# Spreading the attention's reciprocals by DMA through DRAM instead of by TensorE, in a linear-attention and MLP block on one Trainium2 core

## The chip, the cores and the metric

The kernel runs on 1 core of one Trainium2 chip. The metric is the device time of one execution in microseconds (us). Before the change it was 215.84 us, the median of 4 runs (215.45 to 216.13).

The engines are called by the profile's names: PE is TensorE, DVE is VectorE, ACT is ScalarE, POOL is GpSimd, and SP is the engine whose queue issues the DMAs.

## The reference, cut to what matters

```python
# x: 2048 tokens x 640; 32 heads of 20; everything bf16
xn  = layernorm(x)
q, k, v = heads(xn @ wqkv)                    # 32 heads
pq, pk  = phi(q), phi(k)                      # phi(t) = (t > 0 ? t + 1 : exp(t)) + 1e-6
kv  = einsum("bhsd,bhse->bhde", pk, v)
z   = einsum("bhsd->bhd", pk)
num = einsum("bhqd,bhde->bhqe", pq, kv)
den = einsum("bhqd,bhd->bhq", pq, z)[..., None] + 1e-6
out = x + (num / den) @ wo + gelu(xn @ w1 + b1) @ w2 + b2
```

The division is by one number per head and token. The kernel multiplies `pq` by `1/den` before it is used, so each of the 32 reciprocals of a token is needed on 20 partitions of `pqT` (features on partitions, tokens along the row).

## The kernel before: the parts that matter here

PE does, in this order: K, Q and h (the first MLP product) for token groups 0 to 2; K and Q for group 3; G (`xn` transposed times `pk`, 640 x 640) with z, den and the spreading between its parts; h of group 3 with kv, KVW (kv times `wo`) and more spreading between; and the output pass. That pass runs 32 accumulations, each of 12 matmuls of h with `w2` and 5 of `pqT` with KVW.

```python
    # den[32 i + h, s]: denominators of token group i; a reciprocal by Ln and Exp on ACT
    nc.scalar.activation(out=lnden, in_=den[:], func=ACT.Ln, bias=tiny_t[:], scale=1.0)
    nc.scalar.activation(out=recT[:], in_=lnden, func=ACT.Exp, scale=-1.0)

    def emit_pqs(c):                 # spread each reciprocal over the 20 partitions of its head
        rps = [bank() for _ in range(NG)]
        for i in range(NG):
            q = slice(i * H, (i + 1) * H)
            nc.tensor.matmul(
                rps[i][:], lhsT=Em4[q, c * P : (c + 1) * P], rhs=recT[q, :], start=True, stop=True
            )
        for i in range(NG):
            gs = slice(i * TOK, (i + 1) * TOK)
            nc.vector.tensor_tensor(out=pqT[:, c, gs], in0=pqT[:, c, gs], in1=rps[i][:], op=ALU.mult)

    emit_pqs(0)
    emit_Ga(3)                       # G's wide part: 16 matmuls of 512 columns
    emit_pqs(1)
    emit_Gb(3)                       # G's narrow part: 16 matmuls of 128 columns
    ...                              # [cut] pqs(2) in G; h(3), kv, KVW; pqs(3), pqs(4) in h(3)
```

`Em4` is a mask with 32 rows per token group, so the four matmuls of `emit_pqs` each read 32 partitions, where those of G and h read 128 (the trace's forms: 32x512 against 128x512). In the code `P` is 128, `H` the 32 heads, `DH` their 20 features, `NG` the 4 token groups of `TOK` = 512 tokens, `NC` the 5 blocks of 128 features, and `HALF` 320 columns. A bank is a piece of PSUM, the memory that matmuls write to here, and an eviction is the copy of a result out of it. The "products" are the multiplications of `pqT` by the spread reciprocals on DVE.

## Time and profile before

| reading | value | view |
|---|---|---|
| span of the profiled run | 214.0 us | page |
| PE busy | 208.9 us, 98% | page, part 1 |
| chain that ended last, on PE | 95% | page, part 4 |
| PE's waits in total | 2.3 us, all before 9 us | waits of PE |
| end of Q to the output pass | 94.35 to 137.34 us: 42.99 us | chain in order of time |
| granted clock | 1.00 | windows |

From the page of the kernel before: PE's row of part 1, then three rows of part 2, where each digit is the busy share of a fortieth of the span in tenths (PEclk is the granted clock).

```profile
PE 208.9 (98%) x1412; PEld 119.9 (56%) x1412; DVE 100.2 (47%) x249; ACT 83.6 (39%) x135; POOL 60.6 (28%) x82
PE   7799999999999999999999999999999999999994
PEclk9999999999999999999999999999999999999999
DMA  5999970000000000000000000000100110000011
```

PE has no free slice, and the DMA engines are nearly idle after a sixth of the run. So work taken from PE is worth its full time, and DMA has time to give.

The waits of PE, kernel before: engine and line, whom it waited for, total us, times, longest.

```profile
PE mm L183 <- DVE hT L130: 1.1, 1, 1.1
PE mm L272 <- DMA wqk<-in_A_wqkv_dram: 0.9, 1, 0.9
PE mm L248 <- DVE xn L232: 0.3, 1, 0.3
```

All three lie in the start. The chain in order of time, kernel before: start us, us, engine and line, count. L403 is G's wide part, L412 its narrow part, L452 the spreading, L324 is h, and L536 the output pass.

```profile
94.35 3.45 PE mm L403 x16
97.80 0.89 PE mm L412 x16
...
108.81 0.33 PE mm L452 x4
109.14 3.56 PE mm L403 x16
112.70 0.33 PE mm L452 x4
113.03 1.00 PE mm L412 x16
...
132.15 0.33 PE mm L452 x4
132.48 1.19 PE mm L324 x5
...
137.34 1.63 PE mm L536 x12
```

Four spreading matmuls take 0.33 us together. The group behind them is slower than its twins elsewhere: 3.56 instead of 3.45, 1.00 instead of 0.89, 1.19 instead of 1.08 us. The cost of the spreading is therefore not 5 x 0.33 us alone.

### The profile page before, as it was taken

The page shows a single profiled execution, that of the slowest core. Times are in us where ns is not written, and L with a number is a line of the kernel's source. Part 1 is how long each engine was busy: PE and PEld are TensorE (multiplying, and loading weights), DVE is VectorE, ACT ScalarE, POOL GpSimd, SP SyncE. Part 2 cuts the span into 40 slices and gives each one's busy share as a digit, 9 for nine tenths or more (in the row PEclk, how much of TensorE's full clock was granted, in tenths as well). Part 3 has the DMA queues.
Part 4 walks back from the last instruction along what each step waited for, and adds up shares of the span by engine and source line. Part 5 has one row for each costly group of instructions (what it writes and reads, how often), then busy time and mean ns, then how long its engine had stood idle before and what let it go on. Part 6 is the DMA issues. An engine that isn't in the chain of part 4 may idle for free.

```text
span 214.0 us, 3486 instructions
## 1 busy us (share of the span) xinstructions
PE 208.9 (98%) x1412; PEld 119.9 (56%) x1412; DVE 100.2 (47%) x249; ACT 83.6 (39%) x135; POOL 60.6 (28%) x82
## 2 busy tenths in 40 slices
PE   7799999999999999999999999999999999999994
PEld 2454455544554445545554563577777777777762
DVE  4679950999449970794044426612112112112111
ACT  3476769577885869741312736500000000000000
POOL 1000049920550019089899990000000000000000
PEclk9999999999999999999999999999999999999999
DMA  5999970000000000000000000000100110000011
GB/s 175 383 369 312 366 267 5 2 0 0 0 3 0 0 0 3 0 3 0 3 0 0 22 0 0 3 31 31 34 31 31 41 54 31 34 31 31 31 64 31
DMA packets 10079, 12.94 MB, mean 60 GB/s; under 512 B 2304, under 2 KB 8912, under 8 KB 10064
## 3 DMA queue, kind: packets, MB, share of 16 engines
q1 hardware_dynamic: 10064, 12.72, 17.6%
q8 instruction: 11, 0.18, 0.4%
q14 instruction: 4, 0.03, 0.0%
HBM read 10.10 MB, written 2.62 MB: 59 GB/s over the span
## 4 chain that ended last, share of the span: by engine, by line
PE 95%; DMA 3%; SPq 1%; issue 0%; DVE 0%
PE mm L324 24%; PE mm L536 24%; PE mm L540 10%; PE mm L315 10%; PE mm L403 8%; PE mm L272 8%; DMA wqk<-in_A_wqkv_dram 3%; PE mm L412 2%; PE mm L282 2%; PE mm L241 2%; PE mm L452 1%; PE mm L515 1%; PE mm L484 1%; SPq L108 1%; PE mm L439 1%; PE mm L520 0%
## 5 line engine op out<-in xcount | busy, mean ns | idle before, releaser
L536 PE MATMUL mm<-w,hT 128*128 128x320 bf16 (+2 forms) x384 | 57.4, 299 | 0.0
L324 PE MATMUL mm<-xnT,w 128*128 128x512 bf16 x240 | 54.1, 379 | 0.0
L536 PEld LDWEIGHTS <-hT 128*128 128x128 bf16 x384 | 37.1, 98 | 15.3
L544 DVE TENSOR_TENSOR late<-mm,x_all 128x320 bf16<-128x320 f32 (+2 forms) x32 | 15.7, 492 | 58.5 <-PE mm L540 58.5
L328 ACT ACTIVATE hT<-mm,b1col 128x512 bf16<-128x512 f32 x48 | 32.4, 686 | 16.0 <-PE mm L324 15.3
L324 PEld LDWEIGHTS <-w 128*128 128x128 bf16 x240 | 22.8, 98 | 26.6 <-issue 0.7
L256 ACT ACTIVATE e<-mm 128x512 bf16<-128x512 f32 x40 | 23.0, 596 | 12.3 <-PE mm L315 5.4
L540 PE MATMUL mm<-late,pqT 128*128 128x320 bf16 (+2 forms) x160 | 27.0, 299 | 0.0
L257 DVE TENSOR_SCALAR e<-e 128x512 bf16<-128x512 bf16 x40 | 15.0, 374 | 21.5 <-ACT e L256 21.5
L315 PE MATMUL mm<-xnT,wqk 128*128 128x512 bf16 x100 | 22.2, 379 | 0.0
L395 POOL TENSOR_TENSOR x_all<-x_all,b2b 128x640 bf16<-128x640 bf16 x16 | 21.7, 1385 | 0.0
L272 PE MATMUL mm<-wqk,xnT 128*128 128x512 bf16 x80 | 20.4, 379 | 0.9 <-DMA wqk<-in_A_wqkv_dram 0.9
L306 POOL TENSOR_TENSOR zacc<-zacc,pk 128x640 f32<-128x640 f32 x13 | 18.2, 1397 | 7.2 <-DVE pk L260 6.4
L457 DVE TENSOR_TENSOR pqT<-pqT,mm 128x512 bf16<-128x512 bf16 x20 | 12.3, 682 | 14.6 <-PE mm L452 14.6
L540 PEld LDWEIGHTS <-pqT 128*128 128x128 bf16 x160 | 15.5, 98 | 6.3
L403 PE MATMUL mm<-pk,xn 128*128 128x512 bf16 x80 | 18.1, 379 | 0.0
L378 POOL COPY Z3t<-xn 128x1 bf16<-128x1 bf16 x3 | 0.6, 187 | 57.9 <-DVE xn L232 57.9
L315 PEld LDWEIGHTS <-wqk 128*128 128x128 bf16 x100 | 9.6, 98 | 10.8
L196 DVE BATCH_NORM_STATS2 stats<-x_all 128x6 f32<-128x320 bf16 x32 | 13.7, 466 | 3.4 <-DMA x_all<-in_A_x_dram 3.4
L260 DVE SCALAR_TENSOR_TENSOR pk<-mm,e 128x512 bf16<-128x512 f32 x20 | 13.8, 692 | 1.0
L260 DVE SCALAR_TENSOR_TENSOR pqT<-mm,e 128x512 bf16<-128x512 f32 x20 | 13.8, 692 | 0.7
L403 PEld LDWEIGHTS <-xn 128*128 128x128 bf16 x80 | 7.5, 97 | 9.2 <-issue 0.7
(73 smaller groups left out, 132.4 us busy)
## 6 DMA issues: line engine op xcount, KB each, us to landing
w<-in_B_w_dram SPq DMA_DIRECT2D x2, 1920.0 KB, 11.0
out_dram<-late SPq DMA_DIRECT2D x15, 160.0 KB, 1.8
x_all<-in_A_x_dram SPq DMA_DIRECT2D x3, 640.0 KB, 11.1
wqk<-in_A_wqkv_dram SPq DMA_DIRECT2D x1, 800.0 KB, 7.5
wv<-in_A_wqkv_dram SPq DMA_DIRECT2D x1, 800.0 KB
woA<-in_A_wo_dram SPq DMA_DIRECT2D x5, 160.0 KB, 7.4
wqk<-in_A_wqkv_dram SPq DMA_DIRECT2D x1, 480.0 KB, 5.0
x_all<-in_A_x_dram SPq DMA_DIRECT2D x2, 160.0 KB, 2.3
```

The costliest lines, as they stand in the source:

```text
L256: nc.scalar.activation(out=e[:], in_=ps[:], func=ACT.Exp)
L260: nc.vector.scalar_tensor_tensor(out=dst, in0=shaped(ps), scalar=0.0, in1=shaped(e), op0=ALU.max, op1=ALU.add)
L272: nc.tensor.matmul(K_ps[t][:], lhsT=xnT[:, k, t * P : (t + 1) * P], rhs=wqk[:, k, D : D + TOK], start=(k == 0), stop=(k == NC - 1),)
L306: nc.gpsimd.tensor_tensor(out=zsum if u == NT - 1 else zacc[:], in0=pk[:, 0, :] if u == 1 else zacc[:], in1=pk[:, u, :], op=ALU.add,)
L315: nc.tensor.matmul(ps[:], lhsT=wqk[:, k, m * P : (m + 1) * P], rhs=xnT[:, k, gs], start=(k == 0), stop=(k == NC - 1),)
L324: nc.tensor.matmul(ps[:], lhsT=w1[:, k, j * P : (j + 1) * P], rhs=xnT[:, k, g * TOK : (g + 1) * TOK], start=(k == 0), stop=(k == NC - 1),)
L328: nc.scalar.activation(out=hT[g][:, j, :], in_=ps[:], func=ACT.Gelu_apprx_tanh, bias=b1col[:, j : j + 1], scale=1.0)
L395: nc.gpsimd.tensor_tensor(out=x_all[:, t, :], in0=x_all[:, t, :], in1=b2b[:], op=ALU.add)
L403: nc.tensor.matmul(ps[:], lhsT=w, rhs=pk[:, t, 0:TOK], start=(t == 0), stop=(t == NT - 1))
L536: nc.tensor.matmul(ps, lhsT=hT[g][:, j, i * P : (i + 1) * P], rhs=w2[:, j, ns], start=(j == 0), stop=False)
L540: nc.tensor.matmul(ps, lhsT=pqT[:, c, t * P : (t + 1) * P], rhs=KVW[:, c, ns], start=False, stop=(c == NC - 1),)
L544: nc.vector.tensor_tensor(out=osb[:, ns], in0=ps, in1=x_all[:, t, ns], op=ALU.add)
```

## The change

The intent: take the spreading from PE. The reciprocal now goes to DRAM, each row written 20 times by a DMA that reads its source again and again, and comes back as a 640 x 2048 matrix that lies as `pqT` does, into the memory of `xnT`, which is no longer needed then. To have time for that trip, den is computed early, within h of group 3, which moves ahead of G. The rest follows from this: PSUM banks are handed out by hand so that some can be held; z's last adds go to DVE; the reciprocal is a DVE instruction; POOL's 16 bias adds wait (`gate`) for the last product; KVW is made in two halves with held output accumulations between them. The core of the diff, cuts marked:

```diff
+    def emit_den():
+        ...                                        # [cut] the same 20 matmuls as before
+        nc.vector.tensor_scalar(out=zacc[:, 0:TOK], in0=den[:], scalar1=1e-6, scalar2=None, op0=ALU.add)
+        nc.vector.reciprocal(out=recT[:], in_=zacc[:, 0:TOK])
+        for i in range(NG):
+            nc.sync.dma_start(
+                out=rec_rows[:, i * TOK : (i + 1) * TOK].rearrange("(h r) s -> h r s", r=DH),
+                in_=recT[i * H : (i + 1) * H, :].unsqueeze(1).to_broadcast((H, DH, TOK)),
+            )
@@ h of the last group now runs ahead of G
+            if g == 3 and j == 0:
+                emit_zacc(3, nc.vector)
+            if g == 3 and j == 4:
+                emit_z()
+            if g == 3 and j == 5:
+                emit_den()
@@
-    emit_pqs(0)
-    emit_Ga(3)
-    ...                                            # [cut] and all other emit_pqs
+    emit_Ga(0)
+    for c in range(NC):
+        nc.sync.dma_start(out=xnT[:, c, :], in_=rec_rows[c * P : (c + 1) * P, :])
+        nc.vector.tensor_tensor(out=pqT[:, c, :], in0=pqT[:, c, :], in1=xnT[:, c, :], op=ALU.mult)
+    emit_emask()
+    gate(pqT[:, NC - 1, 0:1])                      # a one-element copy on POOL
+    for t in range(NT):
+        nc.gpsimd.tensor_tensor(out=x_all[:, t, :], in0=x_all[:, t, :], in1=b2b[:], op=ALU.add)
+    emit_Gb(0)
+    for j in range(1, NC):
+        emit_G(j)
@@
+    emit_hw(0, halves[0], hold=True)               # 12 matmuls of h with w2 for tile 0
+    emit_KVW(halves[0])
+    emit_hw(0, halves[1], hold=True)
+    emit_KVW(halves[1])
+    emit_hw(1, halves[0], hold=True)
+    emit_hw(1, halves[1], hold=True)
```

## The prediction

> **What bounds it now.** TensorE. The page has PE busy 98% of the 214.0 us span; the chain of waits is 95% PE; the PE waits sum to 2.3 us, all before 9 us. Granted clock is 1.00. A 512-column matmul costs 0.216 us (groups of five, 1.08 us), 320 columns 0.136 us. So only removed PE work, or a new PE wait, moves the time.
>
> **What the change removes, adds, moves.** The denominator's reciprocal is no longer spread over 20 partitions per head by TensorE (mask times recT, 20 matmuls) but by DMA through DRAM: four broadcast writes (2.6 MB), five loads (2.6 MB), five wide DVE products. The last group's h matmuls move ahead of G, den ahead of G too, half of KVW behind first-pass output matmuls; PSUM banks are handed out explicitly.
>
> PE ledger, read from the chain by time. Before, from the end of Q (94.35) to the output pass (137.34): 42.99 us. After, the same work: h 12 x 1.08 = 12.95, z 0.10, den 1.19, G 5 x (3.45 + 0.89) = 21.7, kv 2.06, KVW about 2.2: 40.2. Saved: 2.8 us: 5 x 0.33 us of removed matmuls, and about 1 us because the matmuls after a 32-row group run slower (3.56 instead of 3.45, 1.19 instead of 1.08, 1.00 instead of 0.89). All of it lies on the critical path: floor about 213.1 us.
>
> **What may take it back.**
> 1. den ends near 102.1 us. DVE add 0.7 us, then the reciprocal: not in this trace[...]. Writes start near 106. [...] this trace's loads into 128 partitions made 352 to 382 GB/s (windows view). At about 200 GB/s: 13 us plus latency of about 2 (a 160 KB store takes 1.8 us to land), done near 121; loads at 360 GB/s another 9 us, near 130.5; last product (1.2 us, estimate) near 132. The in-order DVE evicts kv behind these products; PE wants kv near 134.0. Slack only 1 to 2 us; lateness beyond that is lost 1:1.
> 2. woB's loads start when G ends (before: 2.5 us issue plus 1.7 us landing, so 4.2 us); KVW wants them 4.4 us after G: 0 to 0.5 us.
> 3. kv follows G directly, so it waits for G's last eviction on ACT (0.27 us): about 0.3 us.
>
> zsum's four DVE adds (0.82 us each, from 0.49 us at 320 and 0.69 at 512 columns) end near 99.3, before PE wants them at 99.75. The bias adds on POOL (1.385 us each) start late, near 132, but outrun the output pass (2 x 2.31 us a tile).
>
> **Prediction.** 213.6 us, 8 in 10 within 212.6 to 217.0. Faster by over 2%: 0.03; within 2%: 0.90; slower: 0.07.
>
> **What would show it.** Right: PE waits still small after 9 us; removed line gone from PE; output pass ends unchanged; Q ends at 94.35 as before; G near 130.3; 512-column rows at 0.216 us throughout. DMA row busy from about 106 to 131. Wrong on 1: a PE wait of microseconds ahead of the first KVW matmuls, named DVE, with DVE waiting on the load of the spread reciprocal. Wrong on 2: the wait is for the woB DMA.
>
> **What would make it wrong.** Writes well below 200 GB/s (1 KB pieces, 20 readings of a partition) or a slower reciprocal push the time beyond 217; PSUM banks handed out in an unlucky order cost waits inside h or KVW; a PE rate that changes when G runs unbroken.

## The result, and the profile after

The changed kernel took 213.5 us, the median of 10 runs (213.07 to 214.17), against 215.75 us for the kernel before (15 runs, 215.22 to 216.13). The ratio is 0.990, with a 95% interval of 0.9888 to 0.9911. Ratios here are the mean time of one kernel's fast runs over that of the other's of the same rounds, so they are not quite the ratio of the medians quoted. The output is correct. The predicted time was 213.6 us.

The waits of PE after the change are a single line:

```profile
PE bank L180 <- DVE hT L139: 1.1, 1, 1.1
```

The chain in order of time, changed kernel. L318 is den, L353 h, L438 and L447 are G's wide and narrow parts, L487 is kv, L518 is h with `w2`, L537 and L541 are KVW.

```profile
100.41 1.19 PE bank L318 x20
101.61 6.58 PE bank L353 x30
108.19 3.45 PE bank L438 x16
111.64 0.89 PE bank L447 x16
...
129.92 1.40 PE bank L487 x25
131.32 0.66 PE bank L497 x24
131.98 1.74 PE bank L518 x12
133.72 0.68 PE bank L537 x5
134.39 0.37 PE bank L541 x5
134.77 1.74 PE bank L518 x12
...
137.56 3.37 PE bank L518 x24
```

The spreading is gone and G runs at 3.45 and 0.89 us throughout. Four groups are slower than their twins, though, and I had not put that into my sum: h behind den (6.58 us for 30, where 6 x 1.08 = 6.48), and three stretches of h with `w2`, one behind kv's L497 and two behind KVW's L541 (twice 1.74 instead of 1.63, once 3.37 instead of 2 x 1.63 = 3.26 us).

The other side of the bargain is the trip through DRAM. First the DVE timeline of the changed kernel (start us, us, engine, line, operation, tiles, count, idle time before it), then SP's, then three windows (stretch; its length, then for PE, PEld, DVE, ACT and POOL the busy us; granted clock, DMA share, GB/s):

```profile
102.38 3.35 DVE L326 RECIPROCAL recT<-zacc 128x512 bf16<-128x512 f32 x1
125.24 2.46 DVE L463 TENSOR_TENSOR pqT<-pqT,xnT 128x2048 bf16<-128x2048 bf16 x2 [19.50 <-DMA xnT<-rec_rows]
129.29 2.47 DVE L463 TENSOR_TENSOR pqT<-pqT,xnT 128x2048 bf16<-128x2048 bf16 x2 [0.18 <-DMA xnT<-rec_rows]
131.68 0.68 DVE L504 TENSOR_TENSOR late<-bank,zacc 128x512 bf16<-128x512 f32 x1
```

```profile
105.76 6.14 SPq L328 DMA_DIRECT2D rec_rows<-recT  x4
121.13 3.24 SPq L462 DMA_DIRECT2D xnT<-rec_rows  x5
```

```profile
108.00:112.00 4.00, 4.00 (x27) 2.09 (x26) 0.00 (x0) 1.01 (x2) 3.54 (x12) 1.00 0.96 189
112.00:116.00 4.00, 4.00 (x30) 2.11 (x28) 0.00 (x0) 0.26 (x1) 2.50 (x7) 1.00 0.97 209
124.00:128.00 4.00, 4.00 (x32) 2.27 (x30) 2.57 (x3) 1.17 (x2) 0.00 (x0) 1.00 0.98 326
```

The writes go out at 189 to 209 GB/s with the DMA engines 96 to 97% busy, the loads come back at 326. The last product ends at 131.76 us, and the kv eviction (L504) follows at once. PE wants kv at 133.72 us (L537); the eviction of its first four blocks ends at 132.36. The trip fits with 1.36 us to spare.

The start of a run is noisy: in the profiles whose waits were read, PE waited 0 to 1.0 us there for a load of `wqk`. The time from the start of the last eviction to the end of the span varies as well: 2.7 us before the change, 3.2 us after it. For a finer comparison I also give, for each profile, the **inner time**: from the first matmul of Q of group 0 to the start of the last eviction, both read from the chain. The two lines of the kernel before, then the two of the changed kernel:

```profile
14.27 5.39 PE mm L315 x25
211.27 0.29 DVE late L544
13.71 5.40 PE bank L344 x25
208.33 0.29 DVE late L530
```

Before it was 211.27 - 14.27 = 197.00 us, after 208.33 - 13.71 = 194.62 us, so 2.38 us less.

### The profile page after: what moved, and what is told of

Read it like the earlier page. It is cut to its first block, busy times and chain, and to the rows that moved or that the text cites. A ratio compares the mean times of both kernels' runs of the same rounds, so it can differ in the third digit from the quotient of the medians.

```text
span 211.5 us, 3437 instructions
## 1 busy us (share of the span) xinstructions
PE 207.2 (98%) x1392; PEld 120.1 (57%) x1392; DVE 97.1 (46%) x238; ACT 82.7 (39%) x134; POOL 48.5 (23%) x70
## 4 chain that ended last, share of the span: by engine, by line
PE 94%; DMA 2%; DVE 1%; SPq 1%; ACT 0%; issue 0%
PE bank L518 25%; PE bank L353 25%; PE bank L526 10%; PE bank L344 10%; PE bank L438 8%; PE bank L269 7%; DMA x_all<-in_A_x_dram 2%; PE bank L447 2%; PE bank L279 2%; PE bank L238 2%; PE bank L487 1%; PE bank L537 1%; PE bank L318 1%; DVE stats L193 0%; SPq L117 0%; PE bank L541 0%
## 5 line engine op out<-in xcount | busy, mean ns | idle before, releaser
L518 PE MATMUL bank<-w,hT 128*128 128x320 bf16 (+2 forms) x384 | 57.2, 299 | 0.0
L353 PE MATMUL bank<-xnT,w 128*128 128x512 bf16 x240 | 53.7, 379 | 0.0
L518 PEld LDWEIGHTS <-hT 128*128 128x128 bf16 x384 | 36.9, 98 | 15.6 <-issue 0.5
L530 DVE TENSOR_TENSOR late<-bank,x_all 128x320 bf16<-128x320 f32 (+2 forms) x32 | 15.7, 492 | 54.5 <-PE bank L526 54.3
L353 PEld LDWEIGHTS <-w 128*128 128x128 bf16 x240 | 23.1, 98 | 26.8 <-issue 0.4
L357 ACT ACTIVATE hT<-bank,b1col 128x512 bf16<-128x512 f32 x48 | 32.5, 686 | 14.0 <-PE bank L353 13.2
L253 ACT ACTIVATE e<-bank 128x512 bf16<-128x512 f32 x40 | 23.0, 596 | 11.8 <-PE bank L344 7.1
L526 PE MATMUL bank<-late,pqT 128*128 128x320 bf16 (+2 forms) x160 | 26.5, 299 | 0.0
L344 PE MATMUL bank<-xnT,wqk 128*128 128x512 bf16 x100 | 22.2, 379 | 0.0
L467 POOL TENSOR_TENSOR x_all<-x_all,b2b 128x640 bf16<-128x640 bf16 x16 | 21.7, 1392 | 0.0
L269 PE MATMUL bank<-wqk,xnT 128*128 128x512 bf16 x80 | 20.4, 379 | 0.0
L438 PE MATMUL bank<-pk,xn 128*128 128x512 bf16 x80 | 18.1, 379 | 0.0
L257 DVE SCALAR_TENSOR_TENSOR pk<-bank,e 128x512 bf16<-128x512 f32 x20 | 13.8, 692 | 1.0
L438 PEld LDWEIGHTS <-xn 128*128 128x128 bf16 x80 | 7.7, 98 | 8.5
```

The costliest lines, as they stand in the source:

```text
L253: nc.scalar.activation(out=e[:], in_=ps[:], func=ACT.Exp)
L257: nc.vector.scalar_tensor_tensor(out=dst, in0=shaped(ps), scalar=0.0, in1=shaped(e), op0=ALU.max, op1=ALU.add)
L269: nc.tensor.matmul(K_ps[t][:], lhsT=xnT[:, k, t * P : (t + 1) * P], rhs=wqk[:, k, D : D + TOK], start=(k == 0), stop=(k == NC - 1),)
L344: nc.tensor.matmul(ps[:], lhsT=wqk[:, k, m * P : (m + 1) * P], rhs=xnT[:, k, gs], start=(k == 0), stop=(k == NC - 1),)
L353: nc.tensor.matmul(ps[:], lhsT=w1[:, k, j * P : (j + 1) * P], rhs=xnT[:, k, g * TOK : (g + 1) * TOK], start=(k == 0), stop=(k == NC - 1),)
L357: nc.scalar.activation(out=hT[g][:, j, :], in_=ps[:], func=ACT.Gelu_apprx_tanh, bias=b1col[:, j : j + 1], scale=1.0)
```

## The experiments

**Theory A**: what counts is PE work. The removed matmuls and the slower groups behind them make the gain; the order is neutral; the trip is free as long as it ends in time. **Theory B**, its rival: the new order (unbroken h and G, early den, KVW in halves) makes the gain. Further questions were how much slack the trip has, what the one-element copy on POOL is for, and whether theory A can be used again.

| run | median us | ratio to before (95%) | inner time us |
|---|---|---|---|
| before | 215.75 | 1 | 197.00 |
| changed | 213.5 | 0.990 (0.9888 to 0.9911) | 194.62 |
| changed, again | 213.41 | 0.9896 (0.9862 to 0.993) | 194.62 |
| before without spreading, mended | 213.73 | 0.9911 (0.9895 to 0.9927) | 194.83 |
| new order with the old spreading | 215.28 | 0.9972 (0.995 to 0.9994) | 196.80 |
| changed, without KVW's small matmuls | 212.6 | 0.9842 (0.9821 to 0.9864) | 193.66 |
| two more writes | 221.88 | 1.029 (1.0245 to 1.0334) | 202.07 |
| two more writes, DVE order changed | 219.36 | 1.0171 (1.0128 to 1.0215) | 199.58 |
| no gate | 224.57 | 1.0413 (1.0394 to 1.0432) | 206.21 |
| 8 transposes by DMA | 211.24 | 0.9787 (0.9753 to 0.982) | 192.45 |
| 12 transposes by DMA | 210.04 | 0.9744 (0.9719 to 0.9769) | 191.25 |
| 12 transposes, DVE order changed | 209.73 | 0.9733 (0.9706 to 0.976) | 191.25 |

Two runs are not in the table: the spoiled first try (experiment 1), and one more write (experiment 6), whose profile is of a slow run.

### 1. The kernel before without the spreading (first try, spoiled)

```diff
-            nc.tensor.matmul(rps[i][:], lhsT=Em4[q, ...], rhs=recT[q, :], ...)
-            nc.vector.tensor_tensor(out=pqT[:, c, gs], in0=pqT[:, c, gs], in1=rps[i][:], op=ALU.mult)
+            nc.vector.tensor_tensor(out=pqT[:, c, gs], in0=pqT[:, c, gs], in1=recT[:], op=ALU.mult)
```

> The kernel before, with only the 20 spreading matmuls left out (the products take the unspread reciprocal, so the result is wrong on purpose). Theory A, removed TensorE work: 5 x 0.33 us go, and the six matmul groups behind them speed up by 0.11 us each (3.56 to 3.45, 1.00 to 0.89, 1.19 to 1.08), so 2.3 us less than before, about 213.4 us, almost the whole gain of the change. Theory B, the new order (h ahead of G, den early, KVW in halves) made the gain: at most the 1.65 us of the matmuls themselves, 214.1 us or more, and the groups behind keep their times.

It took 222.26 us (220.44 to 223.23), slower than before (ratio 1.0285), with a wrong result as intended. Neither theory foresaw this. The edit had brought in something new: the products now read two operands from SBUF while POOL's bias adds were running (that this is the cause is tested in experiment 5; in the kernel before, with one operand in a bank, twelve products took 0.68 us each under the same adds). The DVE timeline shows twelve of them in 26.05 us:

```profile
105.41 26.05 DVE L451 TENSOR_TENSOR pqT<-pqT,recT 128x512 bf16<-128x512 bf16 x12 [6.57 <-ACT recT L445]
```

One of them lasted 22.2 us, while the median was 0.42 us. POOL's adds ended at 128.15 us, and nine of the twelve ran after that. The kv evictions stood behind them, PE waited 5.3 us for these, and then the granted clock was 0.50 from 132 to 140 us. So the run says nothing about theories A and B. It raised the question that experiment 5 answers, and it was mended:

### 2. The same, with the products left out too

> The first run of this idea kept the products and thereby made VectorE and POOL read SBUF against each other; this is the mended form: the kernel before without the 20 spreading matmuls and without the 20 products behind them (wrong on purpose). Theory A, removed TensorE work: 5 x 0.33 us and five slower followers of 0.11 us go, 2.2 us, about 213.8 us where the kernel before takes 216.0. Theory B, the order makes the gain: 214.3 us or more.

It took 213.73 us against 215.7 us for the kernel before in the same rounds, ratio 0.9911; inner time 194.83, which is 2.17 us less than before. Expected by theory A: 2.2 us, from five slower groups (the first expectation had counted six). G's wide part returns to 3.45 us everywhere but behind z (3.48) and den (3.56). Removing the spreading from the old order yields nearly the whole gain.

### 3. The new order with the old spreading

```diff
-            nc.sync.dma_start(out=rec_rows[...], in_=recT[...].to_broadcast((H, DH, TOK)))   # and the loads
+    for j in range(NC):
+        emit_Ga(j)
+        emit_pqs(j)            # the 20 matmuls and products of the kernel before
+        emit_Gb(j)
```

> The changed kernel with its new order, banks, reciprocal on VectorE and late bias adds, but the reciprocal spread by the 20 matmuls again, four behind each wide G group, no trip through DRAM. Theory A: five times 0.33 us and 0.11 us for the slower group behind come back, 2.2 us, so about 215.7 us, as before. Theory B: the order keeps most of the gain, 213.5 to 214.5 us.

It took 215.28 us, ratio 0.9972. The chain in order of time (L444, L470 and L453 are G's wide part, the spreading and G's narrow part) has what theory A lists:

```profile
112.97 3.45 PE bank L444 x16
116.42 0.33 PE bank L470 x4
116.75 1.00 PE bank L453 x16
```

Five times 0.33 us and 0.11 us came back; from this kernel to the changed one the inner time falls by 2.18 us, and from the kernel before to this one by 0.20 us. So the order by itself is worth about 0.2 of the 2.38 us. The ratio suggests somewhat more (0.6 us), but its interval begins at 0.13 us. Theory B falls.

### 4. What the 0.11 us is

```diff
-            nc.tensor.matmul(ps[:, 0:HALF], lhsT=kv[:, m, :], rhs=woA[:, m, ns], start=True, stop=False)
+            nc.tensor.matmul(ps[:, 0:HALF], lhsT=kv[:, m, :], rhs=woA[:, m, ns], start=True, stop=True)
-        for m, ps in enumerate(pss):
-            nc.tensor.matmul(ps[:, 0:HALF], lhsT=kv[q, NC + a, :], rhs=woB[q, a, ns], start=False, stop=True)
```

> The changed kernel without the ten small matmuls (12 or 32 rows of weights) of KVW, wrong on purpose. Theory A says that a group that follows matmuls on fewer than 128 rows pays 0.11 us: the two output groups behind KVW should fall from 1.74 to 1.63 us, and the time by 2 x (0.37 + 0.11) = 0.96 us, to about 212.5 us. If the 0.11 us has another cause (the wait for KVW's banks, a switch of line), the groups stay at 1.74 and only 0.74 us go, 212.8 us.

It took 212.6 us, and the inner time fell by 0.96 us, the expected figure. The chain of this run:

```profile
132.40 1.74 PE bank L518 x12
134.13 0.68 PE bank L537 x5
134.81 1.63 PE bank L518 x12
136.44 0.68 PE bank L537 x5
137.12 3.26 PE bank L518 x24
```

The group at 134.81 us, no longer behind matmuls of 12 rows, is back at 1.63, and the 24 at 137.12 are at 3.26 instead of 3.37 us. The first stays at 1.74: it stands behind kv's matmuls of 128 x 32 and 128 x 12, which were not touched. The runs give the price here: 0.10 to 0.11 us for the group behind matmuls on fewer rows or columns. They show the price and what it follows, not where it arises: the ends of matmuls in the trace are modelled, so the time could as well be counted as the tail of the small matmuls.

### 5. Without the gate on POOL

```diff
-    gate(pqT[:, NC - 1, 0:1])
```

> The changed kernel without the one-element copy that holds POOL's 16 bias adds behind the last product. The adds then start near 115 us and run 22 us without a gap. In the first run without spreading, nine of twelve products waited until POOL's adds had ended. Theory C, POOL and VectorE exclude each other when both read SBUF this way: the five products start near 137 us instead of 125, the kv evictions near 142, TensorE waits 8 to 10 us before KVW and then runs at half clock for a while: 222 to 228 us. Rival: the gate is only caution, and the time stays 213.5 us.

It took 224.57 us, with a correct result. PE's longest wait, DVE's timeline and POOL's:

```profile
PE bank L536 <- DVE late L503: 9.1, 1, 9.1
125.70 17.16 DVE L463 TENSOR_TENSOR pqT<-pqT,xnT 128x2048 bf16<-128x2048 bf16 x5 [19.24 <-DMA xnT<-rec_rows]
115.59 21.64 POOL L466 TENSOR_TENSOR x_all<-x_all,b2b 128x640 bf16<-128x640 bf16 x16
```

The data were there at 125.70 us, as in the changed kernel. But the first product lasted 12.6 us, until POOL's adds had ended at 137.23; the other four took 1.21 us each. The product got no turn between POOL's adds of 1.4 us, issued without a gap: about eight of them went first. POOL's own adds were not slowed: 16 took 21.64 us here and 21.7 us in the changed kernel. The gate is what makes the change work at all.

The wait explains 9.1 of the 11.59 us of inner time. The windows of this run show the rest:

```profile
136.00:140.00 4.00, 0.00 (x0) 0.00 (x0) 4.00 (x3) 0.00 (x0) 1.23 (x1) 0.78 0.00 0
144.00:148.00 4.00, 4.00 (x19) 1.78 (x18) 0.89 (x2) 1.08 (x3) 0.00 (x0) 0.50 0.02 4
```

PE was granted half its clock from about 138 us, while it still idled, until about 148 us (0.50 also between the two stretches shown, 0.94 in the next four us). The groups that follow took 1.52, 0.64 and 3.13 us instead of 0.68, 0.37 and 1.74, together 2.5 us. The idle PE time was thus paid for twice here: 9.1 us of waiting, and 2.5 us in the groups behind it.

### 6. How much slack the trip has

```diff
+        for i in range(1):     # in the second run: range(2)
+            nc.sync.dma_start(out=spare_rows[...], in_=recT[...].to_broadcast((H, DH, TOK)))
         for i in range(NG):
             nc.sync.dma_start(out=rec_rows[...], in_=recT[...].to_broadcast((H, DH, TOK)))
```

> The changed kernel with one more broadcast write of 640 KB (to a spare DRAM tile) ahead of the four real ones. Its trace says that a write takes 3.5 us, and that the kv evictions, held behind the products, end 1.3 us before TensorE asks for them. Theory: the chain den - reciprocal - writes - loads - products has a slack of 1.3 us and costs 1:1 beyond it: about 2.2 us of wait before KVW, 215.7 us, with that wait named VectorE. Rival: DMA time is hidden by more than that, or by nothing: 213.5 or 217.0 us.

> The same with two more writes, 7.0 us of delay. Theory: a wait of 5.7 us before KVW, 219.2 us; and, as the run with products against POOL showed the granted clock at half for about 9 us after an idle 4.8 us, up to 4.5 us more, so 219 to 224 us. Rival as before: 213.5, or 220.5 at full clock.

One more write: 217.1 us, spread from 215.22 to 220.18. The profiled run, the slowest, was classed as slow (over 1.5% above the fastest of its kernel), so its profile shows only the kind of wait (2.9 us before KVW, named DVE), not a cost to compare. Its three fast runs took 215.22, 216.74 and 217.47 us, the same as before by the ratio (1.0038, 0.9987 to 1.0089). Their mean, 216.5 us, lies between the 215.7 us expected and the 217.0 us of the rival that nothing is hidden, so this run does not decide between the two. Two more writes: 221.88 us. PE waited 5.2 us where 5.7 were expected, and the groups behind took 1.52, 0.64 and 2.91 us instead of 0.68, 0.37 and 1.74, so they lost 2.3 us (the mean granted clock of this run was 0.984); that makes 7.5 us, and the inner time rose by 7.45. Counted from the first matmul of Q, the last product ended 6.5 us later than in the changed kernel, and 6.5 less the 5.2 us of wait leaves 1.3 us. So the slack is real, of the size read from the profile, and in this run what exceeded it was lost more than 1:1.

### 7. Two more writes, but the products behind the kv evictions

```diff
-        nc.vector.tensor_tensor(out=pqT[:, c, :], in0=pqT[:, c, :], in1=xnT[:, c, :], op=ALU.mult)
     ...                                            # G, kv, the three kv evictions
+    for c in range(NC):
+        nc.vector.tensor_tensor(out=pqT[:, c, :], in0=pqT[:, c, :], in1=xnT[:, c, :], op=ALU.mult)
+    gate(pqT[:, NC - 1, 0:1])                      # and the bias adds
-            (nc.vector.tensor_copy if m % 2 else nc.scalar.copy)(out=KVW[:, m, ns], in_=ps[:, 0:HALF])
+            nc.scalar.copy(out=KVW[:, m, ns], in_=ps[:, 0:HALF])
```

> The kernel with two more writes (221.9 us), but with the five products, and the bias adds behind them, placed behind the kv evictions in VectorE's order, and all ten KVW evictions on ACT. If the wait came from VectorE's order alone, not from the DMA traffic, the kv evictions run when their banks are ready, the late products (last one near 139 us) are still ahead of the output pass (near 141 us), and the time is back at 213.5 to 214.2 us. If the traffic itself or anything else cost the time, it stays above 216 us.

A miss: 219.36 us, not 213.5 to 214.2. The wait for DVE did go; another stood behind it. PE's wait and SP's timeline:

```profile
PE bank L548 <- DMA late<-in_A_wo_dram: 2.7, 1, 2.7
128.21 2.51 SPq L468 DMA_DIRECT2D xnT<-rec_rows  x5
130.81 2.58 SPq L482 DMA_DIRECT2D late<-in_A_wo_dram  x5
```

The small loads of `wo`'s remaining rows (woB, 15 to 40 KB each) can start only when G has freed their memory, and here they were issued right behind the late loads of 2.6 MB, on the same queue (q1, which carried 14720 of the run's 14736 packets). By the chain the first of the five kept PE until 6.4 us after its issue, and the one of 40 KB landed 5.9 us after its own; in the kernel before and the changed one that load lands in 1.6 to 1.7 us. Whether they waited for their turn or shared the rate with the late loads (411 GB/s from 132 to 136 us, the DMA engines busy throughout), this run does not show. The inner time rose by 4.96 us. The listed wait is 2.7 of them. Another 0.6 went in the five matmuls behind it, which took 0.98 instead of 0.37 us: by the chain the first starts 0.04 us after its load has landed, and the other four have loads of their own, issued behind that one. The last 1.7 went in the two groups that followed (2.87 instead of 1.74, 1.22 instead of 0.68 us). The granted clock was 0.84 from 136 to 140 us and 0.74 from 140 to 144, 1.00 before and after; if the low clock was 0.50, as in experiment 5, that is from about 138.7 to 142.1 us, an estimate. So a late trip has two ways to hold PE, the order of DVE and the loads issued behind it, and my theory knew only the first. A version with woB in memory of its own, loaded early, would test whether these two are all; it was not run, so that is open.

### 8. The same idea once more: the transposes

If theory A is right, other PE work whose result is not needed at once should be worth its full time too. The tiles of `xn` were transposed on PE, five 128 x 128 matmuls (0.28 us) a tile.

```diff
-            if j > 2 * TPG:
-                emit_T(t1 + j - 2 * TPG - 1, nc.scalar.copy)
+            if g > 0 and TPG <= j < 2 * TPG:       # behind the norm of the tile
+                u = t1 + j - TPG
+                nc.sync.dma_start_transpose(out=xnT[:, :, u * P : (u + 1) * P], in_=xn[:, u, :])
```

> The changed kernel, with the eight tile transposes of token groups 2 and 3 taken from TensorE and made by transposing DMAs as well, at a time when the DMA engines idle. Theory A (any PE work moved to idle DMA is gained whole if its result lands in time): 40 matmuls, 8 x 0.28 us, go; 2.2 us less than the changed kernel, about 211.3 us. The four tiles of a group are normed some 3 to 4 us before K wants the first; if a transposing DMA of 160 KB takes longer than that, PE waits at the first K matmul of groups 2 and 3, and the gain shrinks or turns.

The result was correct, at 211.24 us (ratio 0.9787). Inner time: 2.17 us less than the changed kernel, of 8 x 0.28 = 2.24. No new wait is listed; one group of KVW took 0.76 instead of 0.68 us, because the products of this run ended only just in time. The page's part on DMA issues shows how fast such a transpose lands (count, us from issue to landing):

```profile
xnT<-xn SPq DMA_TRANSPOSE x8, 2.6
```

Group 1 follows in the next run, with the loads that are needed late (b2, wv, wo, w2) issued behind its four transposes:

> The kernel with the transposing DMAs, now for token group 1 too, with the loads that are needed late (b2, wv, wo, w2) issued behind those four. The transposing DMAs landed 2.6 us after issue in the run before; the tiles of group 1 are normed 28.1 to 29.2 us after the start, and K wants the first near 32. By the ledger 4 x 0.28 us more go: 1.1 us below the 211.2 us of that run, about 210.1 us. If the deferred loads or the transposes come late, PE waits ahead of K of group 1, and the time is 211 us or more.

210.04 us, ratio 0.9744; inner time 191.25, which is 3.37 us below the changed kernel, for 12 x 0.28 = 3.36 us of matmuls. Then the DVE order of experiment 7 was put on top of it:

> The same with the products and bias adds behind the kv evictions and KVW evicted by ACT alone. On the median no gain over it, about 210.1 us, as the products there are just in time (0.08 us of a slower group was all that showed); the gain is in the margin: the spread of its runs should be smaller, without runs a microsecond above the median.

209.73 us, ratio 0.9733, the lowest median, though its runs overlap with those before; the inner time is the same 191.25 us. The kv evictions now start at 128.59 instead of 129.89 us, so the margin is larger, but the smaller spread that I expected is not shown (209.47 to 210.23 us, against 209.87 to 210.17 us without it). Last, the changed kernel on the same chip:

> The changed kernel once more, for a comparison on the same chip: 213.5 us, 0.990 of before; first K matmul, end of Q and the time behind the last eviction vary by up to half a microsecond between profiles, with no change of code.

213.41 us, ratio 0.9896. Its inner time is again 194.62 us, while Q of group 0 started at 13.93 us instead of 13.71. Over all profiles that start lies between 13.71 and 14.53 us, with the old code and the new alike. It is noise, and the inner time leaves it out.

## Why the prediction was right, point by point

- **The bound.** Right. PE had no waits after the start, before or after the change, and removed PE time showed up in full in experiments 2, 3, 4 and 8.
- **The saving, "2.8 us".** The mechanism was right and the size a little too large: the inner time fell by 2.38 us. The term that was mis-sized is the "about 1 us" of slower groups. The old order has ten of them, 1.08 us, and I took all of that as saved. Only the five behind the spreading (0.54 us) went with it; the new order still has four: h behind den (6.58 for 6.48) and three stretches of h with `w2` (1.74 for 1.63 twice, 3.37 for 3.26), together 0.43 us. Three small terms, z and h behind it (0.05 us more) and KVW (2.10 for "about 2.2"), nearly cancel, and the rest is rounding: 40.61 us where I had 40.2. Of the 2.38 us, 2.18 belong to the spreading (experiment 3 against the changed kernel) and 0.20 to the order.
- **What may take it back, 1: the trip.** Right. Reciprocal 3.35 us, where the add before it, on 128 x 512 too, took 0.69 us; writes issued from 105.76 us ("near 106"); first load issued, so writes complete, at 121.13 us ("near 121"), at 189 to 209 GB/s; last product ends at 131.76 us ("near 132"); slack 1.36 us ("only 1 to 2 us"). The start near 106 and the 200 GB/s of the prediction were assumptions of mine: the trace of the kernel before has no reciprocal on DVE and no such writes. What sets the rate, the 32 partitions that a write reads, the 1 KB pieces or the repeated reading, no run here tests. "Lost 1:1" was too mild: behind such a wait the granted clock fell to 0.50 in experiment 5 and to 0.74 (mean of 4 us) in experiment 7, and in experiment 6 the groups took 1.7 to 2.2 times as long.
- **2: woB.** No wait in the changed kernel (0 to 0.5 us predicted). Experiment 7 shows the risk I had not seen, that woB is issued behind the late loads and lands late (5.9 us instead of 1.6 to 1.7).
- **3: G's last eviction.** Wrong: kv took 1.40 us before and after, so the 0.3 us did not occur.
- **The sum.** The predicted 213.6 us was a floor of 213.1 plus about half a microsecond of waits. In truth the PE work saved 0.4 us less and the waits were nil. The two errors cancelled, so the median was met more closely than its parts deserve.
- **Not in the prediction at all:** the gate. I read it as a detail, and it decides 11 us.

## What to carry to other kernels

Here, where PE was busy 98% of the time and the DMA engines idle, data movement that PE did with mask or identity matmuls was worth its full time, plus about 0.1 us for each group that followed its matmuls on fewer rows (2.18 us in all for the spreading, 3.37 us for the transposes of twelve tiles), as long as a DMA could do it and be done in time. Before trying the same elsewhere, compute the slack of that trip from the profile first: the order of an engine's work, or of the loads, can turn a late DMA into a PE wait (5.2 us in experiment 6, 2.7 in experiment 7), and PE may pay once more with a lower clock, as it did here behind waits of 2.7 us and more. And before two SBUF operands go to DVE, see what POOL does at that moment: behind POOL's adds a product of 1.21 us took 12.6 us here, and one of 0.42 us took 22.2 us.
